# A causal convolution feeding a two-layer network: paired diagonals, a narrower first convolution, and reordered work ahead of and in the first group

## The chip, the cores and the metric

The kernel runs on one NeuronCore of one Trainium2 chip. Five engines share its on-chip memory and run at the same time, held together by semaphores: TensorE (matrix products), VectorE, ScalarE (both elementwise), GpSimd (here it mostly issues loads that convert to bf16) and SyncE (here it issues stores and transposing transfers). The profile calls them PE, DVE, ACT, POOL and SP; PEld is TensorE's weight load. The metric is the device time of one execution in microseconds. Before the change four runs took 681.1 to 681.47 us, median 681.27.

## What is computed

The input x has 8 sequences of 4096 positions with 192 channels. Each of 8 heads (24 channels) has 7 taps; a softmax over the taps gives the weights of a causal convolution along the sequence. Its result is a matrix of 32768 rows that goes through two products with a leaky ReLU between them.

```python
w = np.exp(weight - weight.max(-1, keepdims=True))
w = w / (w.sum(-1, keepdims=True) + 1e-09)          # 8 heads x 7 taps
y = einsum('hk,bskhg->bshg', w, windows_of(x, 7))   # causal: zeros ahead of the sequence
h = y.reshape(32768, 192) @ w_in                    # 192 x 2048
out = np.maximum(0.01 * h, h) @ w_out               # 2048 x 192
```

## The kernel before

**Tiling.** Two sequences are worked on at once, side by side on the 128 partitions: 64 channels of one above 64 channels of the other. 192 channels are three chunks (c = 0, 1, 2) of 64. A block is 512 positions of such a pair; there are 32 blocks. The first two blocks are cut into halves of 256 positions, so the list `groups` has four small groups and then 30 of 512. Quarters of the first two blocks are numbered q = 0 to 3.

**The steps of a group.** (1) x comes transposed into `xt`, channels on partitions. (2) The convolution gives `yt`. (3) `mm1` multiplies by `w_in`, in units u: for a small group a unit is two slices of 128 hidden channels, three chunks and both sequences, 12 matmuls in 6 places, where a place is two matmuls side by side on the two row halves of the array. ScalarE turns a unit's accumulator `ph` (two buffers) into `g` by a leaky ReLU (L501). (4) `mm2` multiplies `g` by `w_out` (L511 for the small groups, L574 later). The mm2 slots of one group are spread between the mm1 units of the next by the table `plan`; in the very first group there are none.

**Convolution on TensorE.** Nearly all convolutions run on VectorE (L226, L232) while the group before is multiplied. The first group has nobody ahead of it, so its convolution is done by TensorE: a tap is a 64x64 diagonal matrix as weights and a shifted window of `xt` as data (L257). The taps are used as two bf16 parts, p = 0 (high) and p = 1 (the rest), 14 diagonals for each chunk. The sums are divided by the softmax's sum (`rsum`) as they leave PSUM (L271, L276 on VectorE, L452 on ScalarE). `cross=True` sends each sequence's result to the other half of the PSUM partitions, so that a crossed chunk and a straight one together occupy all four 64x64 tiles of the array; `apart=True` uses two banks for it. The order is: chunk 0 with p = 0 alone (7 places, two tiles), chunk 0 with chunk 2 (7, four tiles), chunk 1 with chunk 2 (7, four), chunk 1 alone (7, two). The second group's chunks 0 and 2 are done the same way in the middle of the first group's mm1, 14 places in three pieces after units 1, 3 and 5 (`CUTS`); its chunk 1 is VectorE's.

**Diagonals.** `diag_wide` (L413) multiplies the doubled identity `ident2` (bf16) by float taps `whm`, each tap read 64 times in place; VectorE makes 32 of the 42, ScalarE the other ten, one at a time and all of chunk 1, with `diag_each` (L421).

**Transposes of x.** Quarter 0 is transposed ahead of everything (L179, copied to `xt` by ScalarE at L199). Quarters 1 and 2 are transposed on TensorE from `x_rows` (L188) and copied to `xt` by VectorE (L199): quarter 1 between the first convolution and mm1, quarter 2 after unit 6. Quarter 3 and all later blocks go by transposing DMA on SyncE's queue (L203, L117).

**Weights.** `w_in` lies in two tensors of 1024 columns. Each has three slots: slot 0 is loaded with rows 0 to 127, the lower half of slot 2 with rows 128 to 191. The two row halves of the array need the chunks on their own partitions, so VectorE copies slot 0's upper rows down (`spread_down`, L320) and the lower rows of slots 0 and 2 up (`spread_up`, L323). All these loads, and those of x, are issued by GpSimd one after the other (L314, L148, L346, L152, L99) and move through one queue.

**Order.** The program's text is the order on each engine. What an engine waits for is data and free buffers. PSUM has two double banks for `ph` (tag "ph") and four banks for everything else (tag "po").

Of the kernel before, what the change touches and what calls it, by code (L numbers as in the profile page):

```python
# [10 lines left out]
FP32 = mybir.dt.float32  # L11
BF16 = mybir.dt.bfloat16
# [3 lines left out]
def kernel(  # L16
# [8 lines left out]
    nc = tc.nc  # L25

    B, S, D = x.shape
    H, K = weight.shape
# [3 lines left out]
    BASE = HALO - (K - 1)  # L32
# [3 lines left out]
    CH = 64  # L36
    NCH = D // CH
    ST = 512
# [5 lines left out]
    NBLK = (B // 2) * NB  # L44
    NHALF = 2
    RUN = 4
    NPEC = 3
    FILL = 48
    VK = 4
    FIRST = (0, 2, 1)  # L50
    SKEW = [(c, k) for k in range(2) for c in range(2)]
    pair = iter([(0, 2), (1, 2), (0, 3), (1, 3), (0, 4), (1, 4), (0, 5)])
    for k in range(K):
        SKEW += [(2, k), next(pair)]
    SKEW += [(1, 5), (0, 6), (1, 6)]
    CUTS = {1: (0, 6), 3: (6, 11), 5: (11, 14)}
    GB = 32
    NR = D // (2 * GB)

    const_pool = ctx.enter_context(tc.tile_pool(name="const", bufs=1))  # L60
# [18 lines left out]
    x_nat, x_bf, xt = {}, {}, {}  # L79
# [115 lines left out]
    def evac_first(q, *copies):  # L195
        dst = xt[0][:, :, HALO + q * HT : HALO + (q + 1) * HT]
        dst = dst.rearrange("p c (s k) -> p s c k", s=HS)
        for s, t in enumerate(ptr.pop(q)):
            copies[s](out=dst[:, s], in_=t)  # L199
# [11 lines left out]
    yt = {}  # L211
# [27 lines left out]
    def pe_conv_jobs(grp, c, parts=(0, 1), cross=False, apart=False):  # L239
# [37 lines left out]

        return jobs, evac

    def run(*lists):  # L280
        for slots in zip_longest(*lists, fillvalue=()):
            for both in slots:
                for job in both:
                    job()
# [27 lines left out]
    def load_w_in(n, rows):  # L312
        ps, slot = ((0, 128), 0) if rows == 0 else ((0, CH), 2)
        nc.gpsimd.dma_start(  # L314
            out=w_in[n][ps[0] : ps[1], slot],
            in_=moe_w_in[rows : rows + ps[1], n * WF : (n + 1) * WF],
        )

    def spread_down(n):
        nc.vector.tensor_copy(out=w_in[n][0:CH, 1, :], in_=w_in[n][CH:128, 0, :])  # L320

    def spread_up(n):
        nc.vector.tensor_copy(out=w_in[n][CH:128, 1:3, :], in_=w_in[n][0:CH, 0:3:2, :])  # L323

    def w_in_of(f, e, c, m0, m1):
        n, f = divmod(f, NFC // NPW)
# [6 lines left out]
    load_w_in(0, 0)  # L333
    ident = const_pool.tile([128, 128], BF16)
    make_identity(nc, ident)
    load_w_in(0, 128)
    load_first(1)
    for rows in (0, 128):
        load_w_in(1, rows)
    load_first(2)  # L340


# [60 lines left out]
    cast_first(0, 0, nc.scalar.copy)  # L403
    cast_first(0, 1, nc.scalar.copy, slice(0, 1))
    cast_first(0, 1, nc.vector.tensor_copy, slice(1, 2))
    whm = const_pool.tile([128, NCH, 2, K + 1], FP32, name="whm")
    nc.vector.tensor_copy(out=whm, in_=wps_hm)


    diag = [const_pool.tile([128, 2, K, CH], BF16, name=f"diag{c}") for c in range(NPEC)]  # L410

    def diag_wide(c, p, n):
        nc.vector.tensor_mul(  # L413
            diag[c][:, p, 0:n],
            ident2[:, None, :].to_broadcast([128, n, CH]),
            whm[:, c, p, 0:n, None].to_broadcast([128, n, CH]),
        )

    def diag_each(c, p, ks):
        for k in ks:  # L420
            nc.scalar.activation(  # L421
                out=diag[c][:, p, k, :], in_=ident2,
                func=mybir.ActivationFunctionType.Copy, scale=whm[:, c, p, k : k + 1],
            )


    warm(1, 192)
    transpose_first(0, lambda: select(wps_l, slice(2, 3)))
# [1 line left out]
    warm(1, ST)  # L430
    warm(1, 384)
    evac_first(0, nc.scalar.copy, nc.scalar.copy)
    for p in range(2):
        diag_wide(0, p, K)
    diag_wide(2, 0, K)
    diag_wide(1, 1, VK)
    diag_wide(2, 1, K)
    diag_each(1, 1, range(VK, K))
    diag_each(1, 0, range(K))
    wml = const_pool.tile([128, NCH, K + 1], FP32, name="wml")  # L440
    nc.vector.tensor_add(wml, wps_l, whm[:, :, 1])
    rsum = const_pool.tile([128, NCH, 1], FP32)
    nc.vector.scalar_tensor_tensor(
        out=rsum, in0=wml[:, :, K:], scalar=1e-9, in1=whm[:, :, 0, K:],
        op0=mybir.AluOpType.add, op1=mybir.AluOpType.add,
    )
    nc.vector.reciprocal(rsum, rsum)
    spread_down(0)
    spread_up(0)

    def act_scale(out, in_, scale):
        nc.scalar.activation(  # L452
# [1 line left out]
        )  # L454

    pe_0, evac_0 = pe_conv_jobs(groups[0], 0)
    pe_2, evac_2 = pe_conv_jobs(groups[0], 2, cross=True, apart=True)
    pe_1, evac_1 = pe_conv_jobs(groups[0], 1, (1, 0))
    run(pe_0[:K])
    run(pe_0[K:], pe_2[:K])  # L460
    evac_0(act_scale)
    run(pe_1[:K], pe_2[K:])
    run(pe_1[K:])
    evac_2(act_scale, nc.vector.tensor_scalar_mul)
    evac_1(act_scale)
    transpose_first(1)
    evac_first(1, nc.vector.tensor_copy, nc.vector.tensor_copy)
    wk = const_pool.tile([128, NCH, K], FP32, name="wk")
    nc.vector.tensor_add(wk, whm[:, :, 0, 0:K], wml[:, :, 0:K])
    nc.vector.tensor_mul(wk, wk, rsum.to_broadcast([128, NCH, K]))  # L470


    g, po, acc2, osb, seal = {}, {}, {}, {}, None
# [8 lines left out]
    def mm1(grp, u, M):  # L482
        blk, t0, T = grp
        y = yt[blk]
        nf = ST // T
        ph = psum_h.tile([128, 2, ST], FP32, name="ph", tag="ph")
        chunks = range(NCH) if blk or t0 else FIRST
        for n in range(nf * NCH):
            i, c = n // NCH, chunks[n % NCH]
            f = nf * u + i  # L490
            for e in range(2):
                ps = slice(e * CH, (e + 1) * CH)
                for m in range(0, 128, M):
                    nc.tensor.matmul(  # L494
                        out=ph[m : m + M, e, i * T : (i + 1) * T],
                        lhsT=w_in_of(f, e, c, m, m + M),
                        rhs=y[ps, c, t0 : t0 + T],
                        start=(c == chunks[0]),
                        stop=(c == chunks[-1]),
                    )  # L500
        act = nc.scalar.activation(  # L501
            out=g[blk][:, nf * u : nf * (u + 1), :, t0 : t0 + T],
            in_=ph.rearrange("p e (i t) -> p i e t", i=nf),
            func=mybir.ActivationFunctionType.Prelu, alpha=0.01,
        )
        return act
# [149 lines left out]
    for i, grp in enumerate(groups):  # L656
        blk, t0, T = grp
        steps = T // 64
        if t0 == 0:
            g[blk] = g_pool.tile([128, NFC, 2, ST], BF16, name="g", tag="g")  # L660
        quota = plan.get(i, [16] * 4 if T == HT else [5, 5, 6, 5, 5, 6, 8, 8])

        if i == 0:
            ahead = []
        else:
            ahead = conv_jobs(groups[i + 1]) if i + 1 < len(groups) else []
        per = -(-len(ahead) // steps)
        for j in range(steps):
            early = between.get((i, j), (0, 0))
            for u in range(2 * j, 2 * j + 2):  # L670
                mm2_slots(i, early[u % 2])
                mm1(grp, u, 128 if i <= NSW else CH)
                if i == 0 and u == 0:
                    conv_1 = conv_jobs(groups[1], (1,))
                    for job in conv_1[:3]:
                        job()
                    spread_down(1)
                    spread_up(1)
                    for job in conv_1[3:]:
                        job()  # L680
                    pe_0, evac_0 = pe_conv_jobs(groups[1], 0)
                    pe_2, evac_2 = pe_conv_jobs(groups[1], 2, cross=True)
                if i == 0 and u in CUTS:
                    cut = slice(*CUTS[u])
                    run(pe_0[cut], pe_2[cut])
                if i == 0 and u == 5:
                    evac_0(nc.vector.tensor_scalar_mul)
                    evac_2(nc.vector.tensor_scalar_mul, nc.vector.tensor_scalar_mul)
                if i == 0 and u == 6:
                    transpose_first(2)  # L690
            jobs = ahead[per * j : per * (j + 1)]
            if T == ST:


                jobs = ahead[len(ahead) * j // steps : len(ahead) * (j + 1) // steps]
                for job in jobs:
                    job()
                jobs = []
            mm2_slots(i, quota[j] - sum(early))
            if i == 0 and j == 3:  # L700
                evac_first(2, nc.vector.tensor_copy, nc.vector.tensor_copy)
            if i == 1 and j == 1:
                load_x(3, transpose_x(2))
            for job in jobs:
                job()
            if i == 0 and j == 3:
                transpose_half(3)

            last_half = t0 + T == ST
            if i == NSW and j == steps - 1:  # L710
                evac_o(LAST - 1)
                slot = NSW * NR * NFC
            if j == steps // 4 and last_half and blk > 0:
                load_x(blk + 3)
            if j == steps // 2 and last_half and blk > 0:
                transpose_x(blk + 2)
# [35 lines left out]
```

## Time and profile before

| | |
|---|---|
| runs, median (lowest to highest) | 681.27 us (681.1 to 681.47) |
| profiled execution: time, span | 681.08 us, 679.4 us |
| granted TensorE clock | 1.00 |
| TensorE busy | 675.4 us, 99% |
| ScalarE, VectorE, GpSimd busy | 518.7, 481.3, 146.4 us |
| mm1 (L494), mm2 (L574), mm2 of the small groups (L511) | 377.1, 339.9, 36.8 us |
| first convolution, second (L257) | 5.5 us together |
| first ReLU starts | 10.00 us |

How to read it: the span runs from the first instruction to the last, and the execution's own time has 1.7 us more around it. Matmuls overlap, so that "busy" of TensorE only says that something was in flight; how fast it works is seen from the starts of its matmuls. A line of the timeline has the start, the length, the engine, the source line, the operation, result and inputs, tile and shape, and the count; in brackets the idle time ahead of it and what ended it. A line of the chain has start, length and what.

### The profile page before, as it was taken

Reading aid. Unit: us, or ns where it says so; the run is one execution under the profiler, and the core shown is the slowest. Engines: PE = TensorE matmul, PEld = TensorE weight load, DVE = VectorE, ACT = ScalarE, POOL = GpSimd, SP = SyncE. Lnnn points to the kernel's source line nnn. Section 1 sums busy time; section 2 is a strip of 40 time slices with the busy share of each in tenths; the row PEclk is TensorE's granted clock in tenths of the full one; section 3 lists DMA queues with packets and bytes.
Section 4 is the critical chain, followed back from the end, with each engine's and each line's share of the span. In section 5 each row is a group of like instructions: output and inputs, shape, how many; then the busy total and the mean of one; then the engine's idle time right before and its main releaser. Section 6 shows DMA issues by size and latency. Waiting matters only on the chain.

```text
span 679.4 us, 27093 instructions
## 1 busy us (share of the span) xinstructions
PE 675.4 (99%) x12444; PEld 446.6 (66%) x12444; DVE 481.3 (71%) x811; ACT 518.7 (76%) x608; POOL 146.4 (22%) x205
## 2 busy tenths in 40 slices
PE   9999999999999999999999999999999999999998
PEld 6997666666666666666666666666666666666667
DVE  7989467766768666778667687667786676876612
ACT  8899877777787778777777877778777777777781
POOL 7455210222211222202222112222022220000000
PEclk9999999999999999999999999999999999999999
DMA  9999745656647656646556466565565573321123
GB/s 153 97 116 103 54 79 89 82 64 70 91 78 95 74 55 87 92 76 87 65 64 91 79 94 78 55 84 84 83 87 68 61 96 71 72 56 33 34 49 94
DMA packets 213890, 53.27 MB, mean 78 GB/s; under 512 B 209296, under 2 KB 213392, under 8 KB 213776
## 3 DMA queue, kind: packets, MB, share of 16 engines
q0 software_dynamic: 98752, 13.97, 30.4%
q1 hardware_dynamic: 115008, 37.57, 27.7%
q8 instruction: 97, 1.59, 0.9%
q14 instruction: 17, 0.14, 0.1%
q10 hardware_dynamic: 16, 0.00, 0.0%
HBM read 28.31 MB, written 25.17 MB: 79 GB/s over the span
## 4 chain that ended last, share of the span: by engine, by line
PE 99%; ACT 0%; DVE 0%; issue 0%
PE ph L494 49%; PE acc L574 44%; PE po L511 5%; PE acc L257 1%; PE warm L358 0%; PE ptr L188 0%; ACT xt L199 0%; DVE o_sb L624 0%; PE ptr L179 0%; PE wps L394 0%
## 5 line engine op out<-in xcount | busy, mean ns | idle before, releaser
L501 ACT ACTIVATE g<-ph 128x1024 bf16<-128x1024 f32 x512 | 496.6, 1021 | 140.2 <-PE ph L494 140.0
L232 DVE SCALAR_TENSOR_TENSOR yt<-xt,wk,yt 128x512 bf16<-128x512 bf16 (+1 forms) x582 | 381.5, 729 | 0.2
L494 PE MATMUL ph<-yt,w_in 64*64 64x512 bf16 (+2 forms) x6048 | 377.1, 369 | 0.0
L574 PE MATMUL acc<-g,w_out 64*64 64x512 bf16 x5568 | 339.9, 376 | 0.0
L494 PEld LDWEIGHTS <-w_in 64*64 64x64 bf16 (+1 forms) x6048 | 229.2, 131 | 103.1 <-issue 0.8
L574 PEld LDWEIGHTS <-w_out 64*64 64x64 bf16 x5568 | 178.4, 118 | 118.8
L99 POOL DMA_DIRECT2D x_bf<-in_x_dram x180 | 134.0, 769 | 409.1 <-DMA xt<-x_bf 406.9
L596 DVE STREAM_TRANSPOSE o_t<-acc 128x512 f32<-128x512 f32 x87 | 73.4, 884 | 181.7 <-PE acc L574 181.7
L511 PE MATMUL po<-w_out,g 64*128 64x192 bf16 (+1 forms) x640 | 36.8, 243 | 0.0
L511 PEld LDWEIGHTS <-g 64*128 64x128 bf16 (+1 forms) x640 | 32.6, 95 | 3.2 <-issue 0.4
L226 DVE TENSOR_SCALAR yt<-xt,wk 128x512 bf16<-128x512 bf16 (+1 forms) x97 | 29.6, 332 | 2.9 <-DMA xt<-x_bf 2.7
L584 ACT COPY junk<-junk 128x1 f32<-128x1 f32 x58 | 11.1, 192 | 4.1
L624 DVE COPY o_sb<-po 128x192 f32<-128x192 f32 x8 | 2.8, 356 | 6.8 <-PE po L511 3.9
L257 PE MATMUL acc<-xt,diag 64*64 64x256 bf16 x140 | 5.5, 272 | 0.2 <-ACT xt L199 0.2
L624 ACT COPY o_sb<-po 128x192 f32<-128x192 f32 x16 | 5.1, 324 | 0.3
L257 PEld LDWEIGHTS <-diag 64*64 64x64 bf16 x140 | 4.3, 106 | 1.3 <-issue 0.6
L358 PE MATMUL warm<-const-bfloat16-1.0 128*128 128x512 bf16 (+3 forms) x12 | 3.8, 472 | 0.8 <-PEq L736 0.8
L152 POOL DMA_DIRECT2D x_half<-in_x_dram x6 | 4.3, 730 | 0.7 <-DMA w_in<-in_moe_w_in_dram 0.4
L358 PEld LDWEIGHTS <-const-bfloat16-1.0 128*128 128x128 bf16 x12 | 1.4, 132 | 2.5 <-issue 2.5
L148 POOL DMA_DIRECT2D x_rows<-in_x_dram x4 | 2.9, 733 | 0.0
L413 DVE TENSOR_TENSOR diag<-ident,whm 128x448 bf16<-128x448 bf16 (+1 forms) x5 | 2.6, 580 | 0.0
L421 ACT ACTIVATE diag<-ident,whm 128x64 bf16<-128x64 bf16 x10 | 2.5, 338 | 0.0
(47 smaller groups left out, 23.4 us busy)
## 6 DMA issues: line engine op xcount, KB each, us to landing
out_dram<-o_t SPq DMA_DIRECT2D x112, 192.0 KB, 4.6
x_bf<-in_x_dram POOLq DMA_DIRECT2D x180, 64.0 KB, 3.2
out_dram<-o_sb SPq DMA_DIRECT2D x8, 192.0 KB, 2.9
xt<-x_bf SPq DMA_TRANSPOSE x90, 3.8
w_out<-in_moe_w_out_dram POOLq DMA_DIRECT2D x2, 384.0 KB, 7.8
out_dram<-o_t SPq DMA_DIRECT2D x8, 96.0 KB, 2.2
out_dram<-o_sb SPq DMA_DIRECT2D x8, 96.0 KB, 1.7
w_in<-in_moe_w_in_dram POOLq DMA_DIRECT2D x2, 256.0 KB, 4.8
```

What stands on the lines that cost most here:

```text
L99: ins = nc.gpsimd.dma_start(out=t[:, c, :, e, :], in_=src[2 * rp + e, :, :, c * CH : (c + 1) * CH],)
L226: lambda s=src, d=dst, c=c: nc.vector.tensor_scalar_mul(d, s, wk[:, c, 0:1])
L232: lambda s=src, d=dst, c=c, k=k: nc.vector.scalar_tensor_tensor(out=d, in0=s, scalar=wk[:, c, k : k + 1], in1=d, op0=mybir.AluOpType.mult, ...
L257: lambda k=k, p=p, a=a, ps=ps, to=to, acc=accs[e * apart]: nc.tensor.matmul(out=acc[to, :T], lhsT=diag[c][ps, p, k, :], rhs=xt[0][ps, c, a ...
L358: nc.tensor.matmul(out=wa[:, 0, 0:cols], lhsT=ones[:, 0:128], rhs=ones[:, 0:cols], start=True, stop=True,)
L494: nc.tensor.matmul(out=ph[m : m + M, e, i * T : (i + 1) * T], lhsT=w_in_of(f, e, c, m, m + M), rhs=y[ps, c, t0 : t0 + T], start=(c == chun ...
L501: act = nc.scalar.activation(out=g[blk][:, nf * u : nf * (u + 1), :, t0 : t0 + T], in_=ph.rearrange("p e (i t) -> p i e t", i=nf), func=my ...
L511: return nc.tensor.matmul(out=po[m], lhsT=g[b][ps, fc, e, s * 128 : (s + 1) * 128], rhs=w_out[ps, fc, :], start=start, stop=stop,)
L574: ins = nc.tensor.matmul(out=acc2[gi, r][e * CH : (e + 1) * CH, 0:T], lhsT=w_out_of(ps, fc, r), rhs=g[b][ps, fc, e, t0 : t0 + T], start=fi ...
L584: seal = nc.scalar.copy(out=junk, in_=junk)
L596: nc.vector.transpose(out=osb[gi, 0][:, 0 : T // GB, :, r], in_=acc2.pop((gi, r))[:, 0:T].rearrange("p (j k) -> p j k", k=GB),)
L624: ins = copy(out=o_sb[:, n % 2, :], in_=po.pop(n))
```

## The change

Five things are changed, all in what happens in the first 20 us.

1. The taps are kept as bf16, each written twice in a row (`taps`, 128x96, in place of `whm`, 128x48 float). `diag_wide` reads taps and identity in pairs, all operands bf16 with pairs innermost. It makes all six sets on VectorE, in the order in which they are used; `diag_each` is gone. The small sums (`wml`, `rsum`, `wk`) stand between them.
2. The first convolution: chunks 0 and 1 run together through 14 places. Chunk 2 (`pe_conv_quads`) is cut along its 256 positions into two halves that run on the four tiles together, 14 places of 128 columns. Its crossed half goes to the two banks of `wps`, which held the selected taps.
3. `w_in`'s first half: x's quarter 1 is issued ahead of rows 128 to 191. The downward copy is ScalarE's. The upward copy is split: slot 0 before the convolution's evictions, slot 2 behind them.
4. The first unit of mm1 goes chunk by chunk (chunk 0 for both slices, then 1, then 2). All other units keep slice by slice, the first group's now with chunks in the order 0, 1, 2.
5. The second convolution runs in two pieces of 7 places, after units 1 and 3, and is evicted after unit 3. Quarter 2 is transposed behind unit 5 and copied to `xt` at once, in place of after unit 7.

```diff
-    CUTS = {1: (0, 6), 3: (6, 11), 5: (11, 14)}
+    CUTS = {1: (0, K), 3: (K, 2 * K)}
...
+    def pe_conv_quads(grp, c, crossed):
+        blk, t0, T = grp
+        n = T // 2
+        acc = psum_o.tile([128, ST], FP32, name="acc", tag="po")
+        accs = [(acc, acc), (crossed[:, 0], crossed[:, 1])]
+        jobs = []
+        for p in range(2):
+            for k in range(K):
+                a = BASE + k + blk * ST + t0
+                four = []
+                for h in range(2):
+                    for e in range(2):
+                        ps = slice(e * CH, (e + 1) * CH)
+                        to = slice((e ^ h) * CH, ((e ^ h) + 1) * CH)
+                        four.append(
+                            lambda k=k, p=p, a=a + h * n, ps=ps, to=to, acc=accs[h][e]: nc.tensor.matmul(
+                                out=acc[to, :n], lhsT=diag[c][ps, p, k, :],
+                                rhs=xt[0][ps, c, a : a + n],
...
+        def evac(straight, *scale):
+            y = yt[blk][:, c, t0 : t0 + T]
+            straight(y[:, 0:n], acc[:, :n], rsum[:, c, :])
+            for e in range(2):
...
+                scale[e](y[ps, n:T], crossed[frm, e, :n], rsum[frm, c, :])
...
-    def spread_up(n):
-        nc.vector.tensor_copy(out=w_in[n][CH:128, 1:3, :], in_=w_in[n][0:CH, 0:3:2, :])
+    def spread_up(n, slots=slice(0, 3, 2), copy=nc.vector.tensor_copy):
+        to = slice(slots.start // 2 + 1, (slots.stop - 1) // 2 + 2)
+        copy(out=w_in[n][CH:128, to, :], in_=w_in[n][0:CH, slots, :])
...
-    load_w_in(0, 128)
     load_first(1)
-    for rows in (0, 128):
-        load_w_in(1, rows)
+    for n, rows in ((0, 128), (1, 0), (1, 128)):
+        load_w_in(n, rows)
...
-    whm = const_pool.tile([128, NCH, 2, K + 1], FP32, name="whm")
-    nc.vector.tensor_copy(out=whm, in_=wps_hm)
+    taps = const_pool.tile([128, NCH, 2, K + 1, 2], BF16, name="taps")
+    nc.vector.tensor_copy(
+        out=taps, in_=wps_hm[..., None].to_broadcast([128, NCH, 2, K + 1, 2])
+    )
...
+    def diag_wide(c, p):
+        shape = [128, K, CH // 2, 2]
         nc.vector.tensor_mul(
+            diag[c][:, p].rearrange("p k (m t) -> p k m t", t=2),
+            ident2.rearrange("p (m t) -> p m t", t=2)[:, None].to_broadcast(shape),
+            taps[:, c, p, 0:K, None, :].to_broadcast(shape),
+        )
...
+    diag_wide(0, 0)
+    diag_wide(1, 0)
+    diag_wide(0, 1)
+    nc.vector.tensor_add(wml, wps_l, taps[:, :, 1, :, 0])
+    diag_wide(1, 1)
...
+    diag_wide(2, 0)
     nc.vector.reciprocal(rsum, rsum)
-    spread_down(0)
-    spread_up(0)
+    diag_wide(2, 1)
...
+    spread_down(0, nc.scalar.copy)
+    spread_up(0, slice(0, 1))
...
-    pe_2, evac_2 = pe_conv_jobs(groups[0], 2, cross=True, apart=True)
-    pe_1, evac_1 = pe_conv_jobs(groups[0], 1, (1, 0))
-    run(pe_0[:K])
-    run(pe_0[K:], pe_2[:K])
+    pe_1, evac_1 = pe_conv_jobs(groups[0], 1, cross=True, apart=True)
+    pe_2, evac_2 = pe_conv_quads(groups[0], 2, wps)
+    run(pe_0, pe_1)
     evac_0(act_scale)
-    run(pe_1[:K], pe_2[K:])
-    run(pe_1[K:])
-    evac_2(act_scale, nc.vector.tensor_scalar_mul)
-    evac_1(act_scale)
+    evac_1(nc.vector.tensor_scalar_mul, act_scale)
+    run(pe_2)
+    evac_2(nc.vector.tensor_scalar_mul, act_scale, act_scale)
+    spread_up(0, slice(2, 3))
     transpose_first(1)
...
+        wide = not (blk or t0 or u)
+        order = [(i, c) for i in range(nf) for c in chunks]
+        if wide:
+            order = [(i, c) for c in chunks for i in range(nf)]
...
-                if i == 0 and u == 5:
+                if i == 0 and u == 3:
                     evac_0(nc.vector.tensor_scalar_mul)
                     evac_2(nc.vector.tensor_scalar_mul, nc.vector.tensor_scalar_mul)
-                if i == 0 and u == 6:
+                if i == 0 and u == 5:
                     transpose_first(2)
+                    evac_first(2, nc.vector.tensor_copy, nc.vector.tensor_copy)
...
-            if i == 0 and j == 3:
-                evac_first(2, nc.vector.tensor_copy, nc.vector.tensor_copy)
```

## The prediction

> **What bounds the kernel now.** First the page's busy shares and the chain that ended last.
>
> ```profile
> PE 675.4 (99%) x12444; PEld 446.6 (66%) x12444; DVE 481.3 (71%) x811; ACT 518.7 (76%) x608; POOL 146.4 (22%) x205
> PE 99%; ACT 0%; DVE 0%; issue 0%
> ```
>
> TensorE carries the whole span. A change pays only if TensorE reaches the same work sooner, and what is gained early stays: from 19.3 us on the matmuls follow each other without a gap. So I read the chain over the start, where the edits lie (start, length, what).
>
> ```profile
> 4.44 0.90 ACT xt L199 x2
> 5.34 0.04 issue
> 5.38 3.35 PE acc L257 x84
> 8.73 0.46 PE ptr L188 x12
> 9.18 1.43 PE ph L494 x24
> ```
>
> The first convolution (L257) starts when ScalarE has copied the transposed x, and from then on TensorE alone is the chain: convolution, transposes of the second half block (L188), first two units of mm1 (L494). Next, TensorE's and ScalarE's timelines in the first group, and the weight loads' waits from 5 to 20 us.
>
> ```profile
> 10.55 0.85 PE L257 MATMUL acc<-xt,diag 64*64 64x256 bf16 x24
> ...
> 12.77 0.74 PE L257 MATMUL acc<-xt,diag 64*64 64x256 bf16 x20
> ...
> 14.99 0.52 PE L257 MATMUL acc<-xt,diag 64*64 64x256 bf16 x12
> ...
> 16.22 0.53 PE L188 MATMUL ptr<-ident,x_rows 128*64 128x128 bf16 x12
> ```
>
> ```profile
> 12.22 1.94 ACT L501 ACTIVATE g<-ph 128x1024 bf16<-128x1024 f32 x2 [0.28 <-PE ph L494]
> 14.33 3.02 ACT L501 ACTIVATE g<-ph 128x1024 bf16<-128x1024 f32 x3 [0.17 <-PE ph L494]
> ```
>
> ```profile
> PEld L257 <- DVE diag L413: 0.6, 2, 0.4
> ```
>
> Four interruptions of mm1 are seen. A unit of mm1 is 0.66 us of TensorE, but its leaky ReLU takes 0.92 us of ScalarE from start to start (two end 1.94 after the first starts, one lasts 1.02): in this group, where no second product fills in, ScalarE is almost the bound, resting only 0.28 and 0.17 us. The last row shows TensorE waiting for diagonals.
>
> **Prices from these rows.** One place (two or four 64x64 matmuls of 256 columns side by side) takes 0.109 us: 24 matmuls in 4s are 6 places. Six places of transposes of 128 columns, a pair each, take 0.46 us with the change of tile shape; successive pairs start 0.056 us apart. A change of shape costs about 0.095 us on entering plus 0.025 us at the second place: 0.24 us for one interruption, in and out.
>
> [...] The old diagonals (float scalars, step 0) took 0.62 us for 448 elements and started 0.535 us apart[...]; no row of before shows the doubled form.
>
> **The change, part by part.**
>
> *First convolution.* Before it ran 28 places: 7 with two tiles, 14 with four, 7 with two; start to start 5.38 to 8.57 us, of which 0.13 us are waits beyond 28 x 0.109. After: 14 places with chunks 0 and 1 side by side, then 14 half places (chunk 2, 128 columns, four tiles): 14 x 0.109 + 14 x 0.056 = 2.31 us, end at 7.70. Gain 0.87 us if weights and diagonals keep up. I take 0.056 (the transposes' value); at worst the four loads go two by two and a half place costs 0.109, gaining only 0.13.
>
> *Diagonals.* If paired, [...] 0.30 us start to start. From 4.26: the table (0.25), then (0,0) at 4.54, (1,0) done 5.22, (0,1) 5.52, (1,1) about 5.98, (2,0) 6.38, (2,1) 6.83, with the small sums between. TensorE wants (1,0) at 5.38, (x,1) at 6.14, (2,0) at 6.91, (2,1) at 7.30: no wait. ScalarE loses its ten diagonals (2.49 us), VectorE keeps six. The tap sums for VectorE's convolution (0.35 us) move from 9.77 ahead of it.
>
> *Weight copies.* ScalarE takes the downward one, 1024 columns. Its copies of 192 and 384 columns took 0.352 and 0.512 us, so 0.83 ns a column: 1.04 us. It waits for the first w_in piece (issued 1.86, landed 4.7 later, about 6.54), so runs 6.59 to 7.63. Queued behind it: the convolution's evictions (0.474 each, 0.36 for 128 columns, 0.09 overlapped): chunk 0 done 8.0, chunk 1 8.37, chunk 2 8.90. VectorE: upward copy of slot 0 from 7.17 to 7.59, chunk 1 to 8.08, chunk 2 to 8.44, then slot 2's copy (0.42).
>
> *Loads exchanged on POOL's queue.* Before: w_in rows 128 on issued at 3.08, landing after 4.2, 7.25; x's two at 3.61 and 4.33, landing 7.99 and 8.51. The same bytes in the other order: x at about 7.3 and 7.8, w_in's rows at 8.5. The transposes want x at 7.79, hence a start at about 7.86. Slot 2 is copied 8.55 to 8.97. Later loads keep their place behind the same bytes.
>
> *First unit of mm1 by chunks.* Transposes from 7.86, mm1 from 8.32, chunk 2 wanted at 8.78. It can start at 9.02: slot 2's copy is latest, chunk 2's eviction (8.95) right behind. Stall 0.24. So the second unit starts at 9.25 instead of 9.80: **0.55 us** of the 0.87 arrive. The rest: 0.24 stall, 0.07 waiting for x.
>
> *Second convolution in two pieces, transposes behind unit 5.* TensorE still has 14 places and 6 of transposes, with three interruptions for four: 0.24 us less. But ScalarE then decides. I stepped both orders through with the prices above (unit n+2 needs its accumulator from unit n's ReLU, 1.02 us after that starts). Before: one stall of 0.10 us at unit 5; it ends 0.06 us from the trace. After: the pieces of 7 starve ScalarE 0.4 us each before units 2 and 4, and units 6, 7 and the next group's first then stall 0.07, 0.24 and 0.13 us. Saved 0.24, new stalls 0.44 less the old 0.10: **0.10 us lost**. VectorE gets evictions and the third quarter's copies earlier (about 15.8 and 16.4 against 17.06 and 17.72), so its convolution leads by 1.3 us more; worth nothing, since TensorE nowhere waits for it now. If that lead were gone, slack is about 0.4 us at 46.3 us, where the first full block starts.
>
> Sum: 0.55 - 0.10 = 0.45 us. The profiled execution took 681.08 (span 679.4), so 680.63; the runs' median lies 0.19 higher: **680.8 us**. That is 0.07%, within the 0.2% (1.36 us) that separates a difference from none.
>
> **Rivals.**
> *Diagonals not paired* (the side of slower). For: no row of before shows this pattern. [...] At 0.535 us each, (1,0) comes at 5.69, (1,1) at 6.93, (2,1) at 8.46; the upward copy 8.8 to 9.2, chunk 1's eviction 9.7, chunk 2's 10.1, slot 2 at 10.52. The second unit then starts at 10.8, 1.0 us later than now, and with the 0.1 above: 682.4. It turns from gain to loss when VectorE has lost about 0.45 us over the main case, some 0.38 us each for six instead of 0.30.
> *Half places cost whole ones* (the change doesn't give 21 places). For: eight TensorE instructions per 56 ns, and four loads at a time, are not in the trace. Against: two transposed tiles keep 56 ns, and neighbouring instructions start 3 to 4 ns apart. The convolution ends at 8.44, transposes from 8.53, mm1 at 8.99, chunk 2 at 9.47, second unit 9.69: 0.1 gained, 0.1 lost, 681.3.
> *The rows of w_in come late.* Landing at 9.0 instead of 8.5 puts chunk 2 at 9.52 and the total at 681.3; at 8.5 the copy is already last, so every 0.1 us counts. The same bytes speak against it.
> *No stall at chunk 2*: 680.5.
>
> **How the numbers follow.** Main case 0.60, 680.4 to 681.1; half places whole 0.13; w_in late 0.08; unpaired 0.11; no stall or more found 0.08. Range 680.2 to 681.7: it leaves out most of the unpaired case and a little below. Beyond 1.36 us lies little on either side: the arithmetic ceiling is 0.87 + 0.24 = 1.1 us gained, and the worst single case loses 1.1; two unforeseen things must meet. Faster 0.04, same 0.92, slower 0.04.
>
> **What would show it.** Diagonals of about 0.385 us each, no TensorE wait on them; chunk 2's convolution in about 0.8 us, half places of 0.056; transposes from about 7.9; a gap of some 0.2 us within the first unit, ended by slot 2's copy; second unit near 9.25; ScalarE gaps of 0.4 us before units 2 and 4, then stalls at units 6 and 7. Wrong if diagonals stay at 0.62, if half places take 0.109, or if the gained half microsecond is gone by 19 us for another cause.

## The result: 0.1% slower, and the profile after

| | before | after |
|---|---|---|
| runs together, median | 681.45 us (52 runs) | 682.05 us (34 runs) |
| ratio after / before | | 1.0010, 95% interval 1.0006 to 1.0015 |
| profiled execution: time, span | 681.08, 679.4 us | 681.8, 680.1 us |
| first ReLU starts | 10.00 us | 10.61 us |
| mm1's second unit starts | 9.80 us | 10.31 us |
| same, in the next group | 18.68 us | 19.37 us |

The difference, 0.4 to 1.0 us, is inside the 0.2% that the forecast called no change, but it has the other sign, and the median lies above the range (680.2 to 681.7). The two traces are 0.69 us apart at the second unit of the second group, and 0.7 us at the end: all of it arises in the first 20 us. (A unit's start is that of its first matmul, the 13th of mm1 for the second unit; the timelines below merge these matmuls into longer lines.)

The page of after, busy time of the engines and the chain's shares:

```profile
PE 675.3 (99%) x12472; PEld 455.4 (67%) x12472; DVE 479.7 (71%) x813; ACT 517.6 (76%) x600; POOL 146.4 (22%) x205
PE 98%; DMA 1%; POOL 1%; ACT 0%; DVE 0%; issue 0%; POOLq 0%
```

TensorE's busy time is the same. New is 1% of DMA and 1% of POOL on the chain. Where, is seen in the chain of after over the start (start, length, what):

```profile
3.14 1.38 POOL x_rows L145 x2
4.51 5.16 DMA w_in<-in_moe_w_in_dram
9.67 0.02 issue
9.69 0.43 DVE w_in L357
10.12 0.05 issue
10.17 1.06 PE ph L527 x15
```

Before, TensorE alone carried the chain from 5.38 us on. Now the first convolution isn't on it at all. GpSimd issues x's two loads, then at 4.51 us rows 128 on of `w_in`; these land at 9.67, VectorE copies them up (L357), and TensorE multiplies by them from 10.17. TensorE's timeline of after shows what it did until then:

```profile
5.39 1.73 PE L254 MATMUL acc<-xt,diag 64*64 64x256 bf16 x56 [0.24 <-ACT xt L196]
6.92 0.25 PE L294 MATMUL acc<-xt,diag 64*64 64x128 bf16 x2
...
7.69 0.22 PE L294 MATMUL wps<-xt,diag 64*64 64x128 bf16 x2
8.04 0.75 PE L185 MATMUL ptr<-ident,x_rows 128*64 128x128 bf16 x12
8.73 0.63 PE L527 MATMUL ph<-yt,w_in 64*128 64x256 bf16 x8
9.71 0.30 PE L527 MATMUL ph<-yt,w_in 64*128 64x256 bf16 x1 [0.36 <-DMA w_in<-in_moe_w_in_dram]
10.17 1.06 PE L527 MATMUL ph<-yt,w_in 64*128 64x256 bf16 x15 [0.16 <-DVE w_in L357]
11.16 0.96 PE L254 MATMUL acc<-xt,diag 64*64 64x256 bf16 x28
...
13.49 0.96 PE L254 MATMUL acc<-xt,diag 64*64 64x256 bf16 x28
...
15.81 0.53 PE L185 MATMUL ptr<-ident,x_rows 128*64 128x128 bf16 x12
```

The convolution is as short as forecast: its last matmuls start at 7.69. The transposes follow at 8.04, the first eight matmuls of mm1 at 8.73, and then TensorE stands. It starts one matmul at 9.71, the next at 10.17: between the eighth matmul's start (9.09) and that, 1.08 us have passed. Three interruptions of mm1 remain of four. ScalarE's and VectorE's timelines of after:

```profile
6.45 1.04 ACT L353 COPY w_in<-w_in 64x1024 bf16<-64x1024 bf16 x1 [1.11 <-DMA w_in<-in_moe_w_in_dram]
7.52 0.97 ACT L484 ACTIVATE yt<-acc,rsum 128x256 bf16<-128x256 f32 x2
8.51 0.75 ACT L484 ACTIVATE yt<-wps,rsum 64x128 bf16<-64x128 f32 x2
10.61 1.94 ACT L535 ACTIVATE g<-ph 128x1024 bf16<-128x1024 f32 x2 [1.35 <-PE ph L527]
12.94 1.94 ACT L535 ACTIVATE g<-ph 128x1024 bf16<-128x1024 f32 x2 [0.39 <-PE ph L527]
15.27 4.94 ACT L535 ACTIVATE g<-ph 128x1024 bf16<-128x1024 f32 x5 [0.39 <-PE ph L527]
```

```profile
4.49 0.99 DVE L451 TENSOR_TENSOR diag<-ident,taps 128x448 bf16<-128x448 bf16 x3
...
9.69 0.42 DVE L357 COPY w_in<-w_in 64x1024 bf16<-64x1024 bf16 x1 [1.40 <-DMA w_in<-in_moe_w_in_dram]
```

ScalarE pauses 0.39 us before units 2 and 4, where before showed 0.28 and 0.17. VectorE idles 1.40 us until `w_in`'s rows are there.

### The profile page after: what moved, and what is told of

Its sections match the earlier page's. It is cut to its first block, busy times and chain, and to the rows that moved or that the text cites. A ratio compares the mean times of both kernels' runs of the same rounds, so it can differ in the third digit from the quotient of the medians.

```text
span 680.1 us, 27143 instructions
## 1 busy us (share of the span) xinstructions
PE 675.3 (99%) x12472; PEld 455.4 (67%) x12472; DVE 479.7 (71%) x813; ACT 517.6 (76%) x600; POOL 146.4 (22%) x205
## 4 chain that ended last, share of the span: by engine, by line
PE 98%; DMA 1%; POOL 1%; ACT 0%; DVE 0%; issue 0%; POOLq 0%
PE ph L527 49%; PE acc L608 44%; PE po L545 5%; DMA w_in<-in_moe_w_in_dram 1%; ACT g L535 0%; PE acc L254 0%; POOL x_rows L145 0%; POOL sel L333 0%; POOL w_in L347 0%; DVE w_in L357 0%; DVE o_sb L658 0%; POOL ident masks.py:199 0%; POOL sel L331 0%; POOL ident masks.py:197 0%; POOLq masks.py:199 0%
## 5 line engine op out<-in xcount | busy, mean ns | idle before, releaser
L527 PEld LDWEIGHTS <-w_in 64*64 64x64 bf16 (+1 forms) x6048 | 234.5, 131 | 100.1 <-issue 0.8
L608 PEld LDWEIGHTS <-w_out 64*64 64x64 bf16 x5568 | 182.0, 118 | 115.0
L545 PEld LDWEIGHTS <-g 64*128 64x128 bf16 (+1 forms) x640 | 34.1, 95 | 2.3 <-issue 0.4
L254 PE MATMUL acc<-xt,diag 64*64 64x256 bf16 x112 | 3.7, 271 | 0.2 <-ACT xt L196 0.2
L357 DVE COPY w_in<-w_in 64x1024 bf16<-64x1024 bf16 (+1 forms) x3 | 1.5, 510 | 1.5 <-DMA w_in<-in_moe_w_in_dram 1.4
```

Of the source, the lines that this page charges most:

```text
L254: lambda k=k, p=p, a=a, ps=ps, to=to, acc=accs[e * apart]: nc.tensor.matmul(out=acc[to, :T], lhsT=diag[c][ps, p, k, :], rhs=xt[0][ps, c, a ...
L527: nc.tensor.matmul(out=ph[m : m + M, e, i * T : (i + 1) * T], lhsT=w_in_of(f, e, c, m, m + M), rhs=y[ps, c, t0 : t0 + T], start=(c == chun ...
L545: return nc.tensor.matmul(out=po[m], lhsT=g[b][ps, fc, e, s * 128 : (s + 1) * 128], rhs=w_out[ps, fc, :], start=start, stop=stop,)
L608: ins = nc.tensor.matmul(out=acc2[gi, r][e * CH : (e + 1) * CH, 0:T], lhsT=w_out_of(ps, fc, r), rhs=g[b][ps, fc, e, t0 : t0 + T], start=fi ...
```

## The experiments

Two numbers are read from every trace: the start of mm1's second unit (before 9.80, after 10.31), and the landing of the early loads. The expectations call the theories by letters; A is that the new order of the loads makes the rows late and that this wait is the loss. The 10.42 that the first expectation gives for after's second unit is the start of the matmul behind that first one. Intervals are of 95%, ratios are to before, run alongside each kernel. A trace shows one execution of each kernel. From one profile to the next the landing of the very first load, which no edit but the last touches, moves between 5.76 and 6.80 us, so differences of some tenths between two traces may be chance.

**The order of the loads put back in after.**

```diff
+    load_w_in(0, 128)
     load_first(1)
-    for n, rows in ((0, 128), (1, 0), (1, 128)):
-        load_w_in(n, rows)
+    for rows in (0, 128):
+        load_w_in(1, rows)
```

> The changed kernel with the old load order (w_in's rows 128 on ahead of x's second quarter), nothing else undone. Theory A (the late landing of these rows, 9.67 us instead of the 8.5 us forecast, is the whole loss): the rows land near 7.25, x near 8.5, transposes start near 8.55, mm1 near 9.0, chunk 2 waits for nothing but its eviction (done 9.26), the second unit starts near 9.7 instead of 10.42; the time falls by about 0.7 us below the changed kernel and comes out level with the kernel before (ratio 1.000). Rival B (ScalarE's evictions, which end at 9.26 instead of 8.90, or the order by chunks hold the unit anyway): second unit at 10.2 or later, ratio stays 1.001. Rival C (the queue lags whatever stands in it, because of what the engines do at that time): x lands near 9.6, transposes follow it, second unit near 10.8, ratio 1.0015.

681.58 us, 1.0004 (0.9996 to 1.0012), second unit at 9.79. TensorE's timeline of this run:

```profile
8.65 0.52 PE L185 MATMUL ptr<-ident,x_rows 128*64 128x128 bf16 x11 [0.19 <-DMA x_rows<-in_x_dram]
9.11 1.50 PE L528 MATMUL ph<-yt,w_in 64*128 64x256 bf16 x24
```

The rows land at 7.59, the stall in the first unit is gone, and half a microsecond with it in the trace and in the medians. The interval of the time holds the ratio of after too; it is the trace, with the second unit at 9.79 and not at 10.2 or later, that decides against rival B. But the convolution's gain doesn't appear either: now x lands at 8.61 and the transposes wait for it. (In this execution the convolution also starts 0.23 us later than in after, at 5.62, behind its diagonals; x still comes after its end.) The second unit starts where it did before.

**The order alone, in before.**

```diff
-    load_w_in(0, 128)
     load_first(1)
-    for rows in (0, 128):
-        load_w_in(1, rows)
+    for n, rows in ((0, 128), (1, 0), (1, 128)):
+        load_w_in(n, rows)
```

> The kernel before with only the load order exchanged. Theory A: w_in's rows land near 9.7 here too; VectorE's upward copy (0.76) ends near 10.5, and queued behind it chunk 2's second eviction near 10.95 and x's copies near 11.6; the second unit of mm1 starts near 11.6 instead of 9.80: 1.7 us slower than before, ratio 1.0025. If the bytes alone counted (landing at 8.5, as forecast): copy done 9.3, second unit near 10.4, 0.6 us slower, ratio 1.0009. Rival C (lag from the changed kernel's other work): landing 8.5, as in the line above.

682.63 us, 1.0018 (1.0011 to 1.0024), second unit at 11.27. VectorE's timeline of this run:

```profile
9.66 0.69 DVE L323 COPY w_in<-w_in 64x2048 bf16<-64x2048 bf16 x1 [1.67 <-DMA w_in<-in_moe_w_in_dram]
```

The rows land at 9.64, as in after (9.67), without any of the other edits. The order alone makes them late. It costs more here than in after: the copy has both slots to move, mm1 has started one matmul ahead of it (in after eight, thanks to the order by chunks), and the last eviction of the convolution stands behind the copy on VectorE, from 10.27 to 10.74 us.

**The pieces of the second convolution put back in after** (`CUTS` of three, evictions after unit 5, transposes after unit 6, their copies after unit 7).

> The changed kernel with the second convolution again in three pieces (after units 1, 3, 5) and the third transposes behind unit 6. Theory A: the first unit's stall stays; from the second unit on the first group takes about 0.1 us less (8.88 us instead of 8.95 from the second unit of this group to the second of the next); ratio to before 1.0008 to 1.0009. Rival D (the two pieces and the earlier transposes cost the time): ratio 1.000.

681.89 us, 1.0008 (1.0000 to 1.0016). Rows at 9.88, second unit 10.52. From the second unit to the next group's second unit it is 8.98 us, in after 9.06.

**Both put back.**

> The changed kernel with both the load order and the pieces as before; what stays are the paired diagonals, the 21 places, ScalarE's downward copy and the order by chunks in the first unit. Theory A: as with the load order alone, and 0.1 us less: second unit near 9.7, ratio 0.9998, so about 0.1 us below the kernel before. Rival B: 1.001.

681.43 us, 1.0002 (0.9994 to 1.0011). Second unit 9.84, and from there 8.88 us, against 8.95 in the first experiment. So the two-piece form costs 0.07 to 0.08 us by both pairs of traces; the times can't tell this apart. What is left of the change here (diagonals, 21 places, the downward copy on ScalarE, the order by chunks) ends the convolution early, its last matmuls starting at 7.73, and gains nothing: x's two loads land at 8.16 and 8.66, and the transposes wait for both.

**The wait for the rows taken out of after.** The first two units use slot 0's weights for chunk 2, so that they compute another product; slot 2's copy goes behind the transposes' copies.

```diff
+        if c == 2 and n == 0 and f < 2 * 2 and wide_of[0]:
+            slot = 0
...
-    spread_up(0, slice(2, 3))
     transpose_first(1)
     evac_first(1, nc.vector.tensor_copy, nc.vector.tensor_copy)
+    spread_up(0, slice(2, 3))
```

> The changed kernel, load order and all, but the first two units take slot 0's weights for chunk 2 (other data, so these two units compute another product), and slot 2's upward copy comes behind x's copies. The late rows are then wanted only by the third unit, near 11 us. Theory A (waiting for these rows is the whole loss): transposes and mm1 as in the changed kernel (8.0 and 8.7), chunk 2 held only by its eviction (9.26), second unit near 9.5 instead of 10.3; 0.8 us below the changed kernel, ratio to before 0.9997. Rival B (something else in the first unit): second unit at 10 or later, ratio 1.0005 or more.

```profile
8.49 1.59 PE L532 MATMUL ph<-yt,w_in 64*128 64x256 bf16 x24
```

Both units now run through without a stop. The second starts at 9.19, 1.12 us before after's and 0.06 before the forecast's 9.25. That it is so early, and not near the expected 9.5, is in part luck of this execution: the first piece of `w_in` landed at 6.10 (in after 6.43), and with it ScalarE's copy and evictions came sooner, the last ending at 9.00 in place of 9.26. By the next group's second unit (18.41) 0.27 of the 0.61 us gained on before are left, of which more below. The median is 681.68 us, 1.0001 (0.9993 to 1.0009). The profiled execution, 680.86, was the fastest of the thirteen, and three of them lie below the fastest of the runs of before made alongside (681.05); what holds the others back isn't shown.

**The rows behind the long loads** (order: first piece, second tensor's rows 0 to 127, rows 128 on, x, the rest).

> The changed kernel with the second tensor's rows 0 to 127 in place of x ahead of the rows 128 on (order: first tensor's upper rows, second tensor's upper rows, first tensor's rows 128 on, x, second tensor's rows 128 on). A look at landings: 128 rows of 2 KB take 16 engines about 1.4 us, 64 rows 0.7. If x's short packets make what follows them late, the rows land by the bytes near 8.5; if the 64-row load is late wherever it is third, near 9.5. x lands near 9.8, so transposes and the time come out later (about 1.5 us above the changed kernel).

A single execution took 682.68 us. Rows at 9.09, x at 9.58 and 10.11, second unit 11.29. The rows land between the two cases of the expectation, so that this run alone decides neither. (The expectation's 1.4 us for 128 rows is an estimate that before's trace bears out: there a packet of 2 KB took 173 ns in the median up to 9 us, and eight of them, the share of each of 16 engines if all have the same, make 1.38.)

**The rows between x's two loads.**

> The changed kernel with the rows 128 on between x's two loads. By the bytes: first half of x 7.0, rows 7.7, second half of x 8.4; if what follows x's short packets is late by 1 us: rows near 8.8, x's second half near 9.2. Theory A: in the first case transposes start near 8.45 and the second unit near 9.6, ratio 0.9999; in the second case transposes 9.25, second unit 10.4, ratio 1.001.

682.0 us, 1.0011 (1.0004 to 1.0018). Rows at 8.94, x's second load behind them at 10.71, second unit 12.20. The profiled execution was an unusually long one of this kernel (684.91), and not by the loads alone. Its first 20 us, and below them those of after (stretch, its length, busy time and instructions of PE, PEld, DVE, ACT and POOL, granted clock, DMA share, GB/s):

```profile
0.00:20.00 20.00, 16.45 (x299) 12.02 (x301) 13.05 (x43) 11.83 (x19) 15.51 (x30) 0.91 1.01 137
0.00:20.00 20.00, 18.18 (x352) 13.92 (x354) 15.04 (x51) 14.76 (x22) 16.39 (x31) 1.00 1.05 141
```

The records of the granted clock show 0.5 from 11.56 to 14.97 us and 1.00 before and after, and mm1's pairs of matmuls follow each other every 0.21 us there in place of 0.11. By estimate that is half of 3.41 us, 1.7 us lost. The landings named above came ahead of it. Such executions, with a mean clock of 0.998 or less, are found only in kernels whose TensorE waits long ahead of or in the first unit: 2 of 34 of after (684.06 and 684.87), 3 of 20 here, some in five of the other kernels with late arrivals. There are none among 133 executions of before, nor among the 65 of the five kernels without this wait. What sets it off was not tested; the profile of after itself has 1.00 throughout.

**The rows loaded twice**, to the lower and the upper partitions, in place of slot 2's copy.

```diff
+    for e in range(2):
+        nc.gpsimd.dma_start(
+            out=w_in[0][e * CH : (e + 1) * CH, 2, :], in_=moe_w_in[128:192, 0:WF]
+        )
...
-    spread_up(0, slice(2, 3))
```

> The changed kernel, its load order kept, but the 64 rows from 128 on are loaded twice, once to the lower and once to the upper partitions, one load behind the other; VectorE's copy of slot 2 is dropped. Three readings of why these rows land about 1 us later than the bytes say. Bytes after all (0.7 us each): first load near 8.5, second near 9.2. A fixed delay for what stands behind x's short packets: first 9.5, second 10.2. The 64 rows keep only half of the 16 engines busy, each with 8 packets as in a load of 128 rows: both loads land at about the same time, near 9.6. In the third case chunk 2 starts near 9.65 instead of 10.15, the second unit near 9.85, 0.45 us below the changed kernel, ratio 1.0003; in the second 10.25 and 10.45, ratio 1.0012.

683.1 us, 1.0025 (1.0014 to 1.0036). The lower rows land at 10.46, the upper at 11.10, so that the second unit starts at 11.29. None of the three readings has these landings: the first of the two loads came no sooner, and the second lands 1.0 us after after's copy would have ended (10.11). The time itself is a mixture. Five of the eleven executions, the profiled one among them, have a mean clock of 0.997 or 0.998 and took 684.14 to 685.08 us; in the profiled one the clock is 0.5 from 11.53 to 14.94 us. The other six took 681.75 to 683.1, median 682.36, 0.3 above after's. So most of the 1.05 us by which the whole median lies above after's isn't the extra load's bytes.

**Longer packets for x in after**: each partition takes two neighbouring positions, so that a packet is 768 B in place of 384.

```diff
+            if q == 1:
+                rows = x[0:2, q * HT : (q + 1) * HT, :].rearrange("e (p s) d -> p e s d", s=HS)
```

> The changed kernel with x's second quarter read two positions at a time (each partition takes two neighbouring positions, so packets of 768 B in place of 384 B and half as many; the positions of that quarter come out in another order). In five profiles of the old order the 1160 KB of these four loads are in by 8.5 to 8.8 us, in five of the new order by 9.4 to 10.5. If the short packets ahead of the rows make them late: x lands by 7.6, the rows by 8.8, chunk 2 starts near 9.3 and the second unit near 9.5, ratio 0.9998. If the place in the queue does it whatever the packets: rows near 9.6, second unit near 10.3, ratio 1.001.

681.99 us, 1.0007 (0.9999 to 1.0015). x at 6.97 and 7.83, rows at 10.42, second unit 11.07: the rows are no earlier with half as many packets.

**Why the rows land late: counting packets.** A packet of `w_in` is one row of 1024 columns, 2048 B; nothing else of the early transfers is between 2 and 8 KB. So "under 8 KB" less "under 2 KB" counts the `w_in` rows begun in a stretch. Up to the landing of rows 128 on, 128 + 64 = 192 are due. The DMA view of before from 0 to 7.25 us, and of after from 0 to 9.67 us:

```profile
DMA packets 1136, 0.92 MB, mean 127 GB/s; under 512 B 431, under 2 KB 943, under 8 KB 1136
```

```profile
DMA packets 1498, 1.30 MB, mean 134 GB/s; under 512 B 641, under 2 KB 1153, under 8 KB 1498
```

Before: 1136 - 943 = 193, just those due. After: 1498 - 1153 = 345. When the last of the 64 rows landed, 153 packets of loads issued behind them had already begun. The same count in the other runs:

| run | rows land | begun by then | due |
|---|---|---|---|
| rows ahead of x: order back / both back | 7.59 / 7.53 | 201 / 198 | 192 |
| rows behind long loads | 9.09 | 345 | 320 |
| rows between x's loads | 8.94 | 235 | 192 |
| rows behind x: order only / pieces back | 9.64 / 9.88 | 334 / 341 | 192 |
| rows behind x: wait taken out / longer packets | 9.38 / 10.42 | 330 / 365 | 192 |

So the transfer was not short of throughput: in after 192 packets of this size had ended by 7.99 us, before the forecast's 8.5. Yet the rows landed at 9.67 only; how many of the 192 were theirs the records don't say. For each of these loads the traces also record 16 increments of one semaphore, and the landing is the last of them. For after's rows thirteen come by 8.21 us, the last three at 8.83, 9.54 and 9.67. From the first to the last it is 2.43 us, for before's rows 1.08; over the traces that load these rows whole 1.1 to 1.7 where they are ahead of x, and 2.1 to 3.5 behind x or between its loads. The lag already shows in x: of its 512 packets 500 had begun by 7.25 us, and 15 of the 16 increments of its second load had come by 7.53, but it landed at 8.23. Behind long loads the increments are nearer to each other (25 packets over, 1.7 us). What lags, and why, isn't shown: the packets' records have queue, size and times, but not which of the 16 DMA engines moved them. That x's loads put the rows behind is only suggested by the place in the queue; packet length alone isn't it (with 768 B the rows landed at 10.42). That stays open.

**The other side: what would earlier arrivals give?** In the old order x is what TensorE waits for. Three runs start from "both put back". In the first, the transposes of quarter 1 read the identity in place of x (x is still loaded):

```diff
-                        in_=x_rows[q][:, e, s, c * CH : (c + 1) * CH],
+                        in_=(ident[:, e * CH : (e + 1) * CH] if q == 1
+                             else x_rows[q][:, e, s, c * CH : (c + 1) * CH]),
```

> The kernel with load order and pieces put back, with the second quarter's transposes reading other data (the identity in place of x, so that quarter's output is not the reference's); the load of x itself stays. Theory A': with the old order it is x's landing (8.6) that eats what the narrower convolution gains, as the rows do with the new one. Then the transposes start at 7.85 instead of 8.7, chunk 2 waits for its eviction (9.26) only, the second unit starts near 9.45 instead of 9.84, ratio to before 0.9995. Against it: second unit at 9.8 as before, ratio 1.0002.

681.26 us, 0.9995 (0.9987 to 1.0003). mm1 at 8.34, second unit 9.16: x's landing is what eats the gain in the old order. Yet in the profiled execution (681.54 us) the next group's second unit starts only at 19.11. TensorE's timeline of this run, in the second convolution's second piece:

```profile
12.20 0.30 PE L255 MATMUL acc<-xt,diag 64*64 64x256 bf16 x2
13.24 0.74 PE L255 MATMUL acc<-xt,diag 64*64 64x256 bf16 x18 [0.75 <-issue]
```

Between two matmuls of one piece lie 1.04 us, and no semaphore is waited for ("issue"). The gap is ahead of the 223rd matmul of the program. In the next run, and in the one without the wait for the rows, gaps of 0.37 and 0.16 us lie ahead of the 224th. The DMA records show a transfer of 16 KB on the queue called "instruction" shortly before, and the matmul behind the gap stands after its end by 1.28 us here, 1.33 in the next run, 1.51 without the wait for the rows. Where there is no gap it is 1.64 and more (before 2.20, after 1.93), with one exception, 1.47 behind the long loads. Whether the transfer makes the gap isn't shown; it wasn't tested by itself. Nor does every execution seem to have such a gap: five of this kernel's thirteen took 680.57 to 680.87 us, below the fastest of the 32 runs of before made alongside (681.03).

In the second, the transposes go between chunks 1 and 2 of the first unit, so that x is wanted later:

```diff
+            if wide and (i, c) == (0, NCH - 1):
+                transpose_first(1)
+                evac_first(1, nc.vector.tensor_copy, nc.vector.tensor_copy)
```

> Old load order and three pieces, and the second quarter's transposes stand within the first unit, between chunk 1 and chunk 2, where TensorE waits for the eviction anyway; VectorE takes one more of chunk 2's evictions. x (landing near 8.6) is then wanted at 8.8 only. Theory A': chunk 0 starts near 8.05, chunk 1 near 8.5, transposes 8.85, chunk 2 near 9.3, second unit near 9.55 instead of 9.80 before; ratio 0.9996. If arrivals are not what binds: second unit at 9.8 or later, because of the two more changes of tile shape (0.24), ratio 1.0003.

681.66 us, 1.0002 (0.9994 to 1.0010). Second unit at 9.48, 0.32 before that of before; after the gap the next group's is at 18.79, 0.11 behind it. In this execution the gain is given back.

In the third the first tensor is loaded in two halves of 512 columns, near half, its rows and x first (the loads alone are shown; the copies go by halves too):

```diff
+    load_w_in(0, 0, 0, WF // 2)
...
+    load_w_in(0, 128, 0, WF // 2)
     load_first(1)
     for rows in (0, 128):
+        load_w_in(0, rows, WF // 2, WF)
```

> Like the kernel with both load order and pieces put back, but w_in's first tensor is loaded in two halves of 512 columns: the near half of all 192 rows, then x's second quarter, then the far half. The first two units want only the near half. Copies go by halves too (the far ones behind x's copies), and VectorE takes one more of chunk 2's evictions. By the bytes the near half lands near 5.8 and x near 7.5; ScalarE copies down 5.5 to 6.1 and starts its evictions at 7.1; transposes 7.9, mm1 8.35, chunk 2 evicted by 8.7. Theory A (only arrivals stood between the narrower convolution and its gain): second unit near 9.0 to 9.1 instead of 9.80, ratio 0.9989 to 0.9992. Against it: x lands behind 8.3, or the far half or the second tensor so late that the third or the fifth unit waits (near 10.7, 12.7): ratio 0.9997 or more.

684.19 us, 1.0047 (1.0033 to 1.0060). x landed at 7.28, the earliest of all, and mm1 began at 8.34. Then (waits of this run from 5 to 14 us: total, times, longest)

```profile
PEld L531 <- DVE w_in L356: 3.9, 1, 3.9
DVE w_in L356 <- DMA w_in<-in_moe_w_in_dram: 1.8, 1, 1.8
```

The upward copy of the far half writes two slots in one instruction. mm1's matmuls, which read near columns only, waited for it, while the far rows landed at 12.22. Why readers of near columns had to wait for a copy of far ones isn't shown. On top of that the clock is 0.5 from 11.24 to 18.07 us in this execution; in five of the six its mean is 0.997 or less, and the one at 1.00 took 683.36 us. So this run says little about loads in halves.

In no version here is the median below that of before by more than the intervals allow.

## Why the prediction was wrong, step by step

**The step that failed: "Loads exchanged on POOL's queue".** It took "the same bytes in the other order" to land at the same times, rows at 8.5. They landed at 9.67, and at 9.4 to 10.5 in the six profiles of this order. Followed through the forecast's own sum: the copy ends 1.14 us late (10.11 for 8.97), the second unit starts 1.06 late (10.31 for 9.25). From there to the next group after loses 0.18 us on before where 0.10 was forecast, 0.08 more. The forecast for a profiled execution, 680.63, and these two make 681.77; it took 681.8. That the order of the loads is the cause is shown from both sides: the old order in after takes the stall away (9.79), the new order in before makes the rows late by itself (9.64). With the wait taken out the second unit started at 9.19, in part by the luck named there. x's second load was late too (8.23 for 7.8), but was covered by the rows. The rival "the rows of w_in come late" named what happened, at 9.0 us and with a chance of 0.08: its size was too small and its chance too low, because "the same bytes speak against it" had argued from throughput, and here the last three of 16 increments came 0.6 to 1.5 us behind the thirteenth.

**First convolution: right.** Last matmuls at 7.69 (forecast end 7.70). Half places follow each other every 0.057 us ((7.66 - 6.92) / 13), about half of a whole place's 0.109, so four loads together add next to nothing; the rival of whole places falls.

**Diagonals: right.** Three in 0.99 us, 0.384 each and 0.30 from start to start (forecast 0.385, 0.30), and no wait of TensorE on them within after's convolution. The row from which the forecast read that TensorE waits for diagonals (0.6 us in two waits) said less than that: 0.42 of it is a weight load standing ready at 5.17, ahead of the convolution's start, and only 0.16 us, at 7.11, lie within it. After has such a wait of 0.37 ahead of the start too. The forecast's 0.30 was its author's estimate; before has no multiplication of paired operands. Its rows do say what halving would save: 448 diagonal elements took 0.620 us and 256 took 0.419, by estimate 1.05 ns for each further element, and half of that for 448 is 0.235 us, which from 0.620 leaves 0.385. So the measured 0.384 agrees with half the time per element. The rival of unpaired diagonals, at 682.4 close to the measured time, falls all the same.

**Copies and evictions: partly.** The downward copy took 1.04 us as worked out. Chunk 2's evictions end at 9.26, not 8.90: ScalarE's four start 0.4 to 0.5 us apart, with no overlap. Hidden behind the rows here; with x at hand it would count next: in the trace without the wait for x the last eviction ends at 8.97, and TensorE goes on with chunk 2 at 9.02.

**Two pieces and earlier transposes: right.** Forecast 0.10 us lost; 0.07 and 0.08 by the two pairs of traces, too little for the times to show. ScalarE's pauses of 0.39 before units 2 and 4 (forecast 0.4) and the stalls at units 6 and 7 are there. After is 0.18 us longer than before from the second unit on; the other 0.10 is also in the run with the pieces put back, whose start stalls in the same way, and was not taken apart further.

**The ceiling.** The forecast let 0.55 of 0.87 us arrive. No run got that far and kept it: in the old order x arrives at 8.6, in the new one the rows at 9.7. Take a wait away and 0.6 us appear at the second unit. By the next group 0.27 us of it were left in the profile without the wait for the rows, and less than nothing in the one without the wait for x, because of the gap; some executions of both kernels are faster than any of before made alongside.

## What to carry to other kernels

When loads in one queue are exchanged, don't time the new landings by bytes alone: here a load landed with the last of its 16 increments, 1.46 us behind the thirteenth (8.21 to 9.67), and counting the packets begun by then against those due (345 to 192) showed that throughput was not at fault. Look at the granted clock of each profile before reading its times (0.91 over the first 20 us, with the rows between x's loads, came with 684.91 us against a median of 682.0). A shorter computation ahead of a transfer gains only up to the next arrival, so list the arrivals in order, each with its earliest use, before adding up what a shorter stage is worth. Look also for readers that wait for a copy of columns they don't read: in the run with the halves that was 3.9 us.

## What the hardware showed that was not expected

- When loads behind x's two landed, up to 173 packets of 2 KB more than were due had begun, and 2.1 to 3.5 us passed between the first and the last of their 16 increments; in the one run behind long loads it was 25 packets and 1.7 us.
- In three of the profiles, all of kernels in which TensorE had waited long (2.1, 1.7 and 3.6 us for loads or a copy), the granted clock fell to 0.5 for 3.4 us (twice) or 6.8 us; none of before's 133 executions with a clock on record shows a mean as low as theirs (0.995 to 0.998).
- TensorE paused for up to 1.04 us within one run of matmuls, without a semaphore, at nearly the same place of the program, 1.28 to 1.51 us after the end of a 16 KB instruction transfer.
- Four 64x64 tiles with 128 columns each kept 0.057 us per place, weight loads included.
